# Transposing the attention weights of the last three batches by DMA instead of on TensorE

## The chip, the cores and the metric

The kernel runs on one core of one Trainium2 chip. The metric is the device time of one execution in microseconds (us), lower is better. Executions of one kernel differ by 1 to 2% here, a few by 3%, so kernels are compared only by runs taken in turn on the same chip, and only by those in the fast state (within 1.5% of the fastest of that kernel). A ratio is the mean time of one kernel's fast runs over that of the other's in the same rounds, so it is not quite the ratio of the medians that are quoted.

## The reference, cut to what matters

```python
# 8 batches, 8 heads, 576 positions, 64 channels a head; 32 packed queries a head
p_packed = softmax(p @ k.T / 8) @ v            # [8, 8, 32, 64]
attn = softmax(q @ p_packed.T / 8) @ p_packed  # [8, 8, 576, 64] -> x [8, 576, 512]
x1, x2, x3 = split(x @ w_proj)                 # gates x1, x3; x2 is convolved
y = x1 * irfft(rfft(x2) * rfft(filter)) * x3
out = y @ w_out                                # [8, 576, 512] float32
```

The softmax weights of the second attention (576 positions by 256 packed rows, a batch) are used twice: as they are for the convolution, and transposed for the gates x1 and x3.

## The kernel before: the parts that the change and the argument touch

Every operation is first recorded, then a planner inside the program simulates the engines and fixes the order of each engine's instructions before they are emitted. Its view of a DMA from SyncE (SP): 60 ns of the queue, and a landing some 3 us later. The batches run as a pipeline of four stages; `turn` makes the transposed weights `a2t` and `middle`, one stage later, uses them.

```python
def rates(self):
    if self.dma():
        return 760 if self.engine == "POOL" else 60, 4000 + self.transfer_ns()
...
def turn(b):                       # a2n: softmax product, 4 blocks; a2c: its tail
    ...
    for t in range(2):
        tp = pst(f"a2tp_b{b}", [P, S], FP16)                       # PSUM
        nc.tensor.transpose(tp[:, ds(COL0[4] - 64 * t, P)], a2c, ident[:])
        for i in range(4):
            ...
            nc.tensor.transpose(to, a2n[:, i, ts(t, P)], ident[:])
        nc.vector.tensor_copy(out=a2t[:, t, :], in_=tp[:])
...
def gate(*ms):                     # in middle(b)
    for x, c0 in ((x1, 0), (x3, 2 * DM)):
        for m in ms:
            for t in range(2):
                nc.tensor.matmul(x[:, m - ms[0], :], qm[:, t, ds(c0 + m * P, P)], a2t[:, t, cols],
                                 start=(t == 0), stop=(t == 1))
...
def project_out(n):                # in back(b): five os_b buffers, stores on SP
    ...
    os_ = sb([P, DM], FP32, tag="os", name=f"os_b{b}", bufs=5)
    nc.scalar.mul(out=os_[:], in_=o[:], mul=float(1.0 / SC_Y))
    nc.sync.dma_start(...)         # one to three stores
```

SP already carried four large transposes, those of the queries of batches 4 to 7 (`qT_b<-qn_b`, 16 blocks of 128x128 in one instruction), beside the stores.

The softmax here doesn't subtract the row's maximum and nothing guards it: scores larger than these inputs give would overflow.

## Time and profile before

| | before |
|---|---|
| time, median of three runs | 201.28 us (200.71 to 203.0) |
| span of the profiled execution | 198.3 us |
| PE busy | 184.8 us, 93% of the span |
| transposes of `a2t` on PE | 80, of them 30 in batches 5 to 7 |
| copies of `a2t` on DVE | 16, 0.45 us each |

PE is TensorE, DVE VectorE, ACT ScalarE, POOL GpSimd. The page, the stretches and the chain stand in the prediction below. Two lines are from the tile views of the kernel before, for `qT_b` and for `os_b`. The columns are the number of instructions, the shortest, median and longest time that one held SP (ns), and the first and last start (us).

```profile
L440 SPq DMA_TRANSPOSE qT_b<-qn_b x4: 1937/5840/10869, 73.7 to 112.8; - x4
L440 SPq DMA_DIRECT2D out_dram<-os_b x56: 330/413/772, 52.7 to 194.5; - x56
```

### The profile page before, as it was taken

The numbers are of one execution on the slowest core, as the hardware profiler recorded it, in microseconds if no ns is written. First come the engines' busy times: TensorE is split into PE (matmuls) and PEld (weight loads), VectorE is DVE, ScalarE is ACT, GpSimd is POOL, SyncE is SP. The second block draws the span as 40 slices with busy tenths as digits, with TensorE's granted clock in tenths as the row PEclk, the third lists the DMA queues.
The fourth block names the chain that finished last, engine by engine and source line by source line (L and its number), as shares of the span: only waits on it lengthen the run. The fifth ranks groups of instructions, "written<-read, shape, count | busy, mean of one in ns | idle before, by whom it ended". The sixth has DMA issues, their size and how long they took to land.

```text
span 198.3 us, 5799 instructions
## 1 busy us (share of the span) xinstructions
PE 184.8 (93%) x2413; PEld 114.7 (58%) x2413; DVE 142.2 (72%) x268; ACT 126.4 (64%) x265; POOL 133.5 (67%) x108
## 2 busy tenths in 40 slices
PE   4879989989999999999999999999999999999990
PEld 2226555666765775766665666565756465664630
DVE  4246857998369699966896699668966996798610
ACT  2247567597879978758874878478758556416050
POOL 7404578878566699989966996299529985963100
PEclk9999999999999999999999999999999999999996
DMA  5999999999999999889999999943013103503235
GB/s 136 270 269 197 205 207 198 196 199 195 202 217 268 189 201 179 165 116 244 263 173 156 112 126 201 172 130 85 3 55 107 56 0 118 143 10 132 81 126 141
DMA packets 44843, 30.96 MB, mean 156 GB/s; under 512 B 16336, under 2 KB 39376, under 8 KB 44816
## 3 DMA queue, kind: packets, MB, share of 16 engines
q0 software_dynamic: 29312, 16.52, 60.9%
q1 hardware_dynamic: 14784, 13.34, 28.9%
q10 hardware_dynamic: 720, 0.72, 1.2%
q8 instruction: 19, 0.31, 0.6%
q14 instruction: 8, 0.07, 0.1%
HBM read 35.55 MB, written 9.44 MB: 227 GB/s over the span
## 4 chain that ended last, share of the span: by engine, by line
PE 73%; DVE 8%; DMA 7%; POOL 4%; ACT 3%; issue 1%; ACTq 0%; DVEq 0%; POOLq 0%
PE x_b L440 28%; PE o_b L440 14%; PE f_b L440 7%; DMA kn_b<-in_k_dram 7%; PE fp_b L440 5%; PE s_b L440 4%; DVE tt_b L440 3%; PE kTp_b L440 3%; PE pv_b L440 3%; PE qp_b L440 3%; PE hp L440 2%; DVE zs_b L440 2%; PE a2tp_b L440 2%; PE qTp_b L440 1%; POOL gm_b L440 1%; POOL fa_b L440 1%
## 5 line engine op out<-in xcount | busy, mean ns | idle before, releaser
L440 POOL TENSOR_TENSOR gm_b<-tt_b,tt_b 128x512 f16<-128x512 f32 (+1 forms) x28 | 39.3, 1431 | 5.8 <-DVE tt_b L440 5.3
L440 DVE TENSOR_TENSOR tt_b<-f_b,h 128x1024 f32<-128x1024 f32 x32 | 38.7, 1214 | 4.7 <-PE f_b L440 4.1
L440 PE MATMUL x_b<-a2t_b,qm_b 128*128 128x512 f16 (+1 forms) x256 | 40.9, 286 | 0.2
L440 PE MATMUL x_b<-ac,gm_b 128*128 128x64 f16 (+3 forms) x312 | 36.0, 252 | 0.1
L440 ACT ACTIVATE os_b<-o_b 128x512 f32<-128x512 f32 x36 | 21.4, 597 | 21.8 <-PE o_b L440 21.8
L440 PE MATMUL o_b<-wout,y_b 128*128 128x512 f16 x128 | 33.4, 379 | 0.0
L440 ACT CAST qm_b<-qp_b 128x512 f16<-128x512 f32 x48 | 26.6, 590 | 10.6 <-PE qp_b L440 10.5
L440 POOL TENSOR_TENSOR tt_b<-tt_b,tt_b 128x1024 f32<-128x1024 f32 x12 | 28.3, 2360 | 5.0 <-DVE tt_b L440 4.9
L440 DVE TENSOR_TENSOR w_b<-x1s_b,x_b 128x512 f32<-128x512 f32 (+1 forms) x40 | 24.6, 627 | 8.9 <-ACT x1s_b L440 8.7
L440 ACT COPY x1s_b<-x_b 128x512 f32<-128x512 f32 (+1 forms) x40 | 21.9, 547 | 11.1 <-PE x_b L440 7.7
L440 PEld LDWEIGHTS <-gm_b 128*128 128x128 f16 x312 | 22.3, 98 | 8.8 <-POOL gm_b L440 2.6
L440 POOL TENSOR_TENSOR fa_b<-ez_b 128x512 f16<-128x512 f32 x14 | 17.6, 1273 | 14.2 <-ACT ez_b L440 14.2
L440 PE MATMUL f_b<-qm_b,fa_b 128*128 128x512 f16 x80 | 24.1, 379 | 0.4 <-DVE tt_b L440 0.2
L440 ACT ACTIVATE e_b<-s_b 96x384 f16<-96x384 f32 (+1 forms) x48 | 23.5, 533 | 1.1 <-PE s_b L440 1.0
L440 DVE SCALAR_TENSOR_TENSOR y_b<-w_b,x_b 128x512 f16<-128x512 f32 x32 | 20.6, 681 | 3.9 <-PE x_b L440 3.7
L440 PEld LDWEIGHTS <-a_b 128*128 128x128 f16 x240 | 15.9, 98 | 8.5 <-POOL a_b L440 1.2
L440 PEld LDWEIGHTS <-qm_b 128*128 128x128 f16 x256 | 15.7, 98 | 8.6 <-issue 1.1
L440 POOL TENSOR_TENSOR a_b<-e_b,zr_b 128x1152 f16<-128x1152 f16 (+2 forms) x10 | 17.3, 1735 | 3.5 <-ACT qm_b L440 2.4
L440 PEld LDWEIGHTS <-y_b 128*128 128x128 f16 x128 | 11.9, 98 | 11.5 <-DVE y_b L440 0.6
L440 PE MATMUL kTp_b<-ident,kn_b 96*128 96x96 f16 x192 | 13.0, 205 | 0.9 <-DVE tt_b L440 0.5
L440 PEld LDWEIGHTS <-kn_b 96*128 96x128 f16 x192 | 11.0, 97 | 4.7 <-issue 2.0
L440 ACT COPY ez_b<-fp_b 128x512 f32<-128x512 f32 x16 | 9.4, 586 | 3.7 <-PE fp_b L440 3.4
(78 smaller groups left out, 280.4 us busy)
## 6 DMA issues: line engine op xcount, KB each, us to landing
out_dram<-os_b SPq DMA_DIRECT2D x24, 256.0 KB, 2.7
kn_b<-in_k_dram POOLq DMA_DIRECT2D x8, 576.0 KB, 13.1
vn_b<-in_v_dram POOLq DMA_DIRECT2D x8, 576.0 KB, 14.8
qn_b<-in_q_dram POOLq DMA_DIRECT2D x8, 512.0 KB, 15.1
out_dram<-os_b SPq DMA_DIRECT2D x16, 128.0 KB, 2.4
wp<-in_moe_w_proj_dram POOLq DMA_DIRECT2D x3, 512.0 KB, 18.5
filt<-in_moe_filter_fft_dram SPq DMA_DIRECT2D x4, 256.0 KB, 6.6
out_dram<-os_b SPq DMA_DIRECT2D x16, 64.0 KB, 1.9
```

The source lines that it names most:

```text
L440: ins = op.call(*op.args, **op.kw).ins
```

## The change

The intent: take ten transposes and two copies per batch off the bound engine and VectorE in batches 5, 6 and 7, when the DMA engines have little to do. Each batch's weights are transposed by twelve DMAs on the SP queue.

```diff
-    TURNED = 4
+    TURNED, TURNED_K, TURNED_A = 4, 9, 5
...
-        for t in range(2):
+        for t in range(2) if b >= TURNED_A else ():
+            for i in range(4):
+                for r, c in ((slice(0, P), COL0[i]),) if i != 2 else ((slice(0, 64), 320), (slice(64, P), MAIN)):
+                    nc.sync.dma_start_transpose(a2t[:, t, c:c + r.stop - r.start], a2n[r, i, ts(t, P)])
+            nc.sync.dma_start_transpose(a2t[:, t, ds(COL0[4], 64)], a2c[64 * t:64 * t + 64, :])
+        for t in range(2) if b < TURNED_A else ():
             tp = pst(f"a2tp_b{b}", [P, S], FP16)
```

The rest of the diff offers the same for the keys from batch `TURNED_K` = 9 on, which no batch reaches.

More of the change, by code (lines that the diff above doesn't have):

```diff
@@ L665, in q_tail @@
                                       in_=tp[:, :, c].rearrange("p g (r e) -> p g e r", e=2))
-        k_turn(0)
-        yield 260
+        for g in range(4) if b >= TURNED_K else ():
+            nc.sync.dma_start_transpose(kTr[g][:, 0:6 * KP].rearrange("p (x r) -> p x r", r=KP),
+                                        kn[:, 2 * g:2 * g + 2, :].rearrange("p h x -> p (h x)"))
+        if b < TURNED_K:
+            k_turn(0)
+            yield 260
         pack()
         yield 230
-        k_turn(1)
-        yield 260
+        if b < TURNED_K:
+            k_turn(1)
+            yield 260
         score1(0)
         yield 270
-        k_turn(2)
-        yield 260
+        if b < TURNED_K:
+            k_turn(2)
+            yield 260
         score1(1)
         yield 270
-        k_turn(3)
-        yield 260
+        if b < TURNED_K:
+            k_turn(3)
+            yield 260
         score1(2)
```

## The prediction

> **What bounds the kernel now.** I first read the page: the totals by engine, the forty slices, the chain of work that ended last.
>
> ```profile
> PE 184.8 (93%) x2413; PEld 114.7 (58%) x2413; DVE 142.2 (72%) x268; ACT 126.4 (64%) x265; POOL 133.5 (67%) x108
> ...
> PE   4879989989999999999999999999999999999990
> ...
> PEclk9999999999999999999999999999999999999996
> DMA  5999999999999999889999999943013103503235
> ...
> PE 73%; DVE 8%; DMA 7%; POOL 4%; ACT 3%; issue 1%; ACTq 0%; DVEq 0%; POOLq 0%
> ```
>
> TensorE (PE) is busy in 93% of the span, at full clock, and from the fourth slice on it is hardly ever free; the chain that ends last runs through it for 73% of the time. The other engines have room on average. The DMA row matters too: the engines are full until about slice 26 (129 us), while the inputs are loaded, and almost idle after that.
>
> A busy figure does not say that PE is the limit exactly where the change acts, so I then cut the span at the starts of the softmax products (tile a_b: 117.8 us for batch 5, 137.5 for batch 6, 158.2 for batch 7, from the timeline of GpSimd).
>
> ```profile
> 97.40:117.80 20.40, 20.31 (x290) 13.02 (x289) 16.12 (x30) 15.08 (x34) 16.70 (x14) 1.00 1.35 158
> 117.80:137.50 19.70, 19.23 (x275) 12.34 (x275) 15.95 (x30) 13.79 (x30) 14.23 (x11) 1.00 0.76 150
> 137.50:158.20 20.70, 20.54 (x277) 12.62 (x275) 16.20 (x28) 14.54 (x32) 14.22 (x10) 1.00 0.16 52
> 158.20:176.70 18.50, 18.50 (x166) 11.59 (x166) 14.86 (x22) 8.49 (x16) 14.04 (x10) 1.00 0.25 74
> ```
>
> The columns are the stretch and its length, the busy time of PE, PE's weight loads, VectorE (DVE), ScalarE (ACT) and GpSimd (POOL), the clock, and the share and rate of DMA. In the stretches of batches 5 to 7 PE idles for 0.5, 0.2 and 0.0 us. So what leaves PE's queue there shortens the kernel by nearly its own length. There is one hole to fill: at 132.6 to 136.5 us the chain leaves PE for DVE.
>
> ```profile
> 132.17 0.45 PE f_b L440 x2
> 132.64 0.69 DVE gm_b L440
> 133.33 0.36 DVE a2t_b L440
> 133.69 1.27 DVE zs_b L440
> 135.02 0.26 issue
> 135.28 1.17 DVE tt_b L440
> 136.49 0.42 PE kTp_b L440 x6
> ```
>
> One of the copies that the change removes (a2t_b) stands in that piece of DVE work.
>
> **What the Trainium skill says.** (1) "TensorE: Matmul & The Clock Gate", Part 4: PE-mode transpose, gives about 390 ns for a 128x128 transpose alone and about 275 ns within a kernel, with a copy out of PSUM to follow. The trace has a mean of 219 ns here, but that is its length from start to end; back to back, only the distance between starts counts, and it is 56 ns (below). The measurement decides. (2) "VectorE: DVE Perf Modes", The three transpose paths, puts the DMA way at 1309 ns for 128x128. No run yet has such a piece alone; the trace has four large ones. (3) "DMA: Bandwidth & Descriptors", Rules for kernel authors, says that transfers under 64 KB pay mostly overhead. The pieces are 32 KB and 16 KB. The trace agrees as far as it goes: output stores of 64 to 256 KB all hold the SP queue for about 0.4 us and land after some 2 us. (4) The same page, DMA Transpose (X-bar), warns of two queues transposing at once; here every one is on SP, so nothing is added to serialize them.
>
> **The change part by part.** The line with TURNED_K = 9 is inert, since no batch number reaches 9; the keys stay on PE. Only the three batches 5, 6 and 7 of the attention weights move.
>
> ```profile
> L440 PE MATMUL a2tp_b<-ident,a_b 128*128 128x128 f16 x80 | 7.4, 219 | 0.0
> L440 DVE COPY a2t_b<-a2tp_b 128x576 f16<-128x576 f16 x16 | 7.1, 450 | 4.4 <-PE a2tp_b L440 4.4
> qT_b<-qn_b SPq DMA_TRANSPOSE x4, 10.9
> ```
>
> Removed from PE: ten transposes per batch, thirty in all. In the PE timeline a group of five starts at 132.44 and the next matmul at 132.72, so five cost 0.28 us and one 56 ns. Thirty times 56 ns is 1.7 us, all in stretches where PE is the limit.
>
> Removed from DVE: two copies per batch, six in all; 6 x 0.45 is 2.7 us of DVE. DVE is some 80% busy in these stretches, so most of that is worth nothing; I count only the hole, 0.36 us on the chain for batch 5. Two PSUM banks per batch come free as well, which I count as nothing.
>
> Added on SP: twelve transposes per batch, 36 in all. What one holds SP is an estimate: an output store holds it 0.41 us in the median, and the one whole-batch transpose that ran after the others' traffic had eased took 1.94 us for 16 blocks of 128x128, 0.12 us a block. So a piece takes some 0.33 + 0.12 = 0.45 us, twelve take 5.4 us. That same large transpose landed 4.3 us after its start, 2.4 us after SP had issued it. Hence all twelve have landed about 7.8 us after the first is issued. The DMA engines' own work is small: it moved 512 KB in about 4 us; a batch is 288 KB.
>
> Is this hidden? For each batch I compare the end of the softmax product with the first gate matmul that reads a2t. Batch 5: product done at 119.9, but SP is held by the last query transpose until 123.65; 123.7 + 7.8 is 131.5, with five output stores of 0.4 us in between 133.5; needed at 137.3. Batch 6: 139.6 + 7.8 is 147.4; needed at about 155.5. Batch 7: 160.3 + 7.8 is 168.1; needed at 171.7. All three have slack, 3.8, 8 and 3.6 us, so the latency lies beside other work.
>
> Moved: the emitted order of all instructions is planned by the program itself before it is built, so removing operations reshuffles it, perhaps from the start. The planner takes 60 ns of SP and a landing some 3 us after the start for such a piece, less than I estimate.
>
> Added on PE: the gate matmuls now wait on several DMA completions instead of one DVE copy; the completions rotate over few semaphores (the trace shows eight for SP). Where an instruction cannot carry all its waits, extra semaphore instructions stand before it. If six per batch cost 50 ns each (what they cost SP in this trace) and none is hidden, that is 0.9 us over three batches; I expect half, 0.4 us.
>
> Sum: -1.7 (PE) - 0.4 (hole) + 0.4 (waits) = -1.7 us. The base is 201.3 us as a median of three that lie 2.3 us apart; the profiled execution took 200.05 us. I take 201.2 as the base and predict 199.5 us.
>
> **Rivals.** First, the pieces land late and the gates wait for them. For it: the query transposes landed after 14 and 18 us while inputs were being loaded, and the plan assumes quicker pieces than I do, so it may pull gates to where their data is not yet there. Against it: DMA is at 0.16 and 0.25 of capacity in batches 6 and 7, and the last load lands at 123 us, before batch 5's pieces can start. It would cost 1 to 3 us in each of one or two batches and make 201 to 205 us.
>
> Second, SP becomes the bound: stores stand behind twelve pieces, the five os_b buffers fill, ScalarE waits and PE with it. For it: 5.4 us of SP in one block, and each issue waits for the landing of the eighth before it. Against it: SP is idle for 8 to 10 us in each stretch (135.5 to 145.9, 153.8 to 163.8), just after the products end, and one batch fills only four or five os_b buffers. It would make 200 to 203 us.
>
> Third, more gain than the instructions removed: with a2t ready 2 to 5 us earlier and without PSUM, gate matmuls can fill holes such as that of 132.6 to 136.5 us. In the three stretches PE has 0.7 us free and perhaps 1 us more in the last 22 us, so it would make 198 us, hardly less.
>
> Fourth, pieces into one tile are held one after another, each waiting for the landing of the one before: 12 x 2.4 us is 29 us per batch and the end would slip by 15 to 20 us. Against it: the second query transpose was issued at 79.4, before the first had landed at 81.1, and the pieces write disjoint columns. I give it 3%.
>
> **Range and chances.** A change of -1.7 us is -0.8%, and the medians themselves wander by half a per cent. Rival three sets the low end, 198.0; rivals one and two the high end, 202.3. Faster by over 2% needs 197.2 us, more than twice the PE time removed: 6%. Slower by over 2% needs 205.3, a stall in two batches or rival four: 7%. The rest, 87%, is within 2%.
>
> **What would show it.** PE should have 2383 matmuls less any change in filler ones, with ten a2tp transposes in each of batches 0 to 4 only, and DVE ten a2t copies instead of sixteen. SP should show 40 transposes, 36 of them about 0.45 us long, landing within 2 to 3 us. The stretch between softmax products should be about 0.5 us shorter in the last batches. I am wrong if the waits list PE behind a DMA into a2t_b for more than 1 us, if pieces hold SP far longer than 0.45 us, or if ScalarE's os_b waits for SP's stores. If the time falls by 3 us or more, the worth of PE's 56 ns was not the main term.

## The result, and the profile after

| | before | after |
|---|---|---|
| median | 201.0 us | 212.35 us (210.08 to 215.02) |
| ratio of the fast runs | | 1.0527, 95% interval 1.0414 to 1.0639 |

The kernel became 5% slower, outside the stated range. The first profile fell in the slow state (215.0 us), so the changed kernel was run once more, unedited, for a profile of a fast execution: 210.29 us, beside 210.1 us of the two fastest runs above. All lines of the changed kernel are of that second profile. What stood on record for it:

> The changed kernel once more, unedited, for a profile in the fast state (the one in hand is of the slow state, 215.0 us). Expected 210 to 212 us, SP held 1.22 us by each of the 36 pieces, 15 us per batch, PE waiting for a2t three times for 8 to 10 us in all, and the granted clock at half in one stretch after each wait over 3 us. If the wait for a2t is absent in a fast run, the slow state explained the wait and not the change.

The page: busy times, then PE, the clock granted to it and the DMA engines in forty slices, and the chain that ended last.

```profile
PE 187.5 (90%) x2383; PEld 114.8 (55%) x2383; DVE 140.1 (67%) x262; ACT 126.5 (61%) x265; POOL 133.5 (64%) x108
...
PE   4889989999999999999999969998994799799990
...
PEclk9999999999999999999999988999999589999997
DMA  5999999999999999999999995113601341047325
...
PE 50%; SPq 18%; DMA 10%; DVE 8%; POOL 5%; ACT 3%; issue 3%; ACTq 0%; DVEq 0%; POOLq 0%
```

The counts are as predicted: PE has 2383 matmuls in place of 2413, DVE 262 instructions in place of 268. The order that the planner gave PE is unchanged for its first 1737 matmuls. But PE now has holes late in the kernel, the clock falls there, and SP's queue, absent from the chain of before, holds 18% of it. The DMA engines themselves have room there (0.58, 0.29 and 0.25 of capacity in the stretches below). The same cut as in the prediction, at the softmax products of this run (117.5, 140.9 and 161.7 us; the last stretch ends where batch 7's gates have found their data), with the columns named there:

```profile
117.50:140.90 23.40, 20.78 (x265) 12.68 (x264) 15.71 (x28) 14.56 (x32) 14.22 (x11) 0.93 0.58 98
140.90:161.70 20.80, 17.42 (x250) 10.63 (x250) 14.33 (x24) 13.34 (x29) 14.23 (x11) 0.99 0.29 78
161.70:182.00 20.30, 17.77 (x125) 9.48 (x125) 11.45 (x16) 7.90 (x15) 11.56 (x8) 0.85 0.25 68
```

PE was free for 0.5, 0.2 and 0.0 us in the stretches of before; here it is free for 2.6, 3.4 and 2.5 us. Who released it, from the view of waits (total, times, longest):

```profile
PE x_b L440 <- DMA a2t_b<-a_b: 6.4, 3, 4.1
```

That is a gate matmul waiting for the transposed weights, once in each of the three batches (6.4 us in all, less than the 8 to 10 that were expected). Why they are late stands in SP's queue: how long a piece holds it (tile view of `a2t_b`), and its order in time (start, length, what).

```profile
L440 SPq DMA_TRANSPOSE a2t_b<-a_b x36: 1121/1226/2130, 125.7 to 182.1; - x36
```

```profile
125.72 17.01 SPq L440 DMA_TRANSPOSE a2t_b<-a_b  x12
142.83 5.23 SPq L440 DMA_DIRECT2D out_dram<-os_b  x8
148.60 15.68 SPq L440 DMA_TRANSPOSE a2t_b<-a_b  x12
164.39 3.12 SPq L440 DMA_DIRECT2D out_dram<-os_b  x6
167.62 15.68 SPq L440 DMA_TRANSPOSE a2t_b<-a_b  x12
```

A piece holds SP for 1.23 us in the median, not 0.45, whether it has 128 rows or 64, and twelve hold it for 16 to 17 us. From 125.7 to 183.3 us SP is never free for longer than 0.6 us: from one batch's first piece to the next batch's it takes 22.9 and 19.0 us, where the kernel before had 19.7 and 20.7 us for a batch in all. So pieces are late for the gates, and they begin late too: those of batch 5 behind a query transpose, those of batches 6 and 7 behind the stores of the batch before.

The waits cost more than their length. "TensorE: Matmul & The Clock Gate", Why this matters for your kernels, in the Trainium skill, says that a gap of more than about 3 us between matmuls sends TensorE back to the slow clock. The longest wait of this trace agrees: from 161.1 us on, within the wait of 4.1 us that ends at 163.0, the clock is granted at one half for 6.8 us, while in the kernel before it fell only at the very end. (Not every gap agrees; see pieces_unused and the last section.) The columns are those of the stretches above; the clock is the third from the end.

```profile
161.12:167.94 6.82, 4.97 (x24) 2.33 (x25) 0.69 (x1) 1.66 (x3) 2.70 (x2) 0.50 0.39 118
```

Not all of this profile's loss is shown to be the change's: at 120.7 us PE idles for 1.9 us for no reason that the profile names, and 3.4 us at half clock follow; this gap is most of the 2.6 us of the first stretch above. The slow profile of the same kernel has no such gap, but waits of 9.9 us for `a2t` and three stretches of 3.4 us at half clock, each beginning between 0.5 us before and 1.4 us after the end of such a wait.

An estimate from these numbers: 6.4 us of waits, 2.5 us for the work done at half clock after them (half of 4.97), 1.9 us of the unexplained gap and 1.7 us for the half clock after it make 12.5 us. The span grew by 10.1 us although some 1.5 us of work was taken away (nothing_added below), so 11.6 us are to be explained.

### The profile page after: what moved, and what is told of

The parts are those of the page before. It is cut to its first block, busy times and chain, and to the rows that moved or that the text cites.

```text
span 213.2 us, 5781 instructions
## 1 busy us (share of the span) xinstructions
PE 188.9 (89%) x2383; PEld 115.7 (54%) x2383; DVE 140.1 (66%) x262; ACT 126.3 (59%) x265; POOL 133.4 (63%) x108
## 4 chain that ended last, share of the span: by engine, by line
PE 51%; SPq 20%; DMA 9%; DVE 7%; POOL 5%; ACT 3%; issue 2%; ACTq 0%; DVEq 0%; POOLq 0%
PE x_b L440 20%; SPq L440 20%; PE o_b L440 8%; DMA kn_b<-in_k_dram 7%; PE f_b L440 4%; PE s_b L440 3%; PE fp_b L440 3%; PE kTp_b L440 3%; DVE tt_b L440 3%; DMA a2t_b<-a_b 2%; POOL tt_b L440 2%; PE hp L440 2%; PE qp_b L440 2%; PE pv_b L440 2%; PE qTp_b L440 1%
## 5 line engine op out<-in xcount | busy, mean ns | idle before, releaser
L440 PE MATMUL x_b<-a2t_b,qm_b 128*128 128x512 f16 (+1 forms) x256 | 42.9, 291 | 9.9 <-DMA a2t_b<-a_b 9.9
L440 PE MATMUL x_b<-ac,gm_b 128*128 128x64 f16 (+3 forms) x312 | 38.9, 264 | 0.1
L440 PEld LDWEIGHTS <-gm_b 128*128 128x128 f16 x312 | 23.8, 102 | 10.6 <-issue 2.4
L440 POOL TENSOR_TENSOR fa_b<-ez_b 128x512 f16<-128x512 f32 x14 | 17.6, 1269 | 13.9 <-ACT ez_b L440 13.9
L440 PE MATMUL f_b<-qm_b,fa_b 128*128 128x512 f16 x80 | 24.8, 387 | 0.4 <-DVE tt_b L440 0.2
L440 PEld LDWEIGHTS <-a_b 128*128 128x128 f16 x210 | 13.8, 98 | 7.3 <-POOL a_b L440 1.2
L440 PE MATMUL kTp_b<-ident,kn_b 96*128 96x96 f16 x192 | 14.5, 217 | 1.0 <-DMA kn_b<-in_k_dram 0.5
L440 PEld LDWEIGHTS <-kn_b 96*128 96x128 f16 x192 | 12.1, 104 | 5.4 <-issue 2.6
```

What stands on the lines that cost most here:

```text
L440: ins = op.call(*op.args, **op.kw).ins
```

## The experiments

Twelve runs; nothing_added gave wrong output. The medians are of all runs, the ratios of the fast ones to those of the kernel before, in the same rounds.

| run | edit | median us | ratio (95% interval) |
|---|---|---|---|
| sizes | kernel before, ten DMAs after its end | 227.0 | - |
| nothing_added | transposes taken away, none put in | 198.91 | 0.9927 (0.9877 to 0.9977) |
| merged7 | seven pieces for twelve | 198.46 | 0.9927 (0.9857 to 0.9996) |
| pieces_unused | pieces issued, result not used | 206.16 | 1.0321 (1.0249 to 1.0392) |
| after_again | changed kernel | 210.29 | one run |
| only_last | batch 7 alone | 204.09 | 1.0170 (1.0083 to 1.0258) |
| kept_warm | PE kept busy in the waits | 208.27 | 1.0396 (1.0325 to 1.0466) |
| told_plan | planner told 1270 ns | 208.82 | 1.0414 (1.0322 to 1.0506) |
| stores_on_act | stores issued by ScalarE | 228.16 | 1.1341 (1.1252 to 1.1430) |
| whole | one transpose per batch, 5 to 7 | 198.93 | 0.9941 (0.9915 to 0.9968) |
| whole_from4 | the same from batch 4 | 198.35 | 0.9929 (0.9903 to 0.9956) |
| whole_from1 | the same from batch 1 | 202.58 | 1.0130 (1.0091 to 1.0169) |

The theory, A: a transposing DMA costs SP a fixed time per instruction, so twelve small pieces fill SP's queue, and everything behind it is late. Rivals are named with each run.

### What one transpose costs SP (sizes)

```diff
+    nc.vector.tensor_copy(out=scr[:, 0:DM], in_=last[0][:])        # scr, dst: dead query tiles
+    for n in (1, 1, 2, 4, 8, 9, 16):
+        nc.sync.dma_start_transpose(dst[:, 0:n, :], scr[:, 0:n * P])
+    nc.sync.dma_start_transpose(dst[:, 0, 0:64], scr[0:64, 0:P])
+    nc.sync.dma_start_transpose(dst[:, 0, 0:32], scr[0:32, 0:P])
+    nc.sync.dma_start(dst[:, 0, :], scr[:, 0:P])
```

> The kernel before with ten further DMAs on SP after its last store, one at a time (all write one dead tile, so each waits for the landing of the one before): transposes of 1, 1, 2, 4, 8, 9 and 16 blocks of 128x128, then one of 64 rows, one of 32 rows, and a plain copy of 128x128. It is there to be measured, not to be fast (some 30 us longer). Theory A (a fixed cost per transposing instruction): the one-block pieces hold SP 1.1 to 1.25 us, the 64-row and the 32-row one as long, nine blocks 1.4 to 1.7 us, sixteen 1.9 us. Rival B (cost by the block): one block 1.2 us, two 2.4 us, sixteen far over the 1.94 us seen in the kernel before, or else the 64-row piece half of the 128-row one. Rival C (back-pressure by earlier pieces in flight): alone, one block takes 0.4 to 0.5 us and only pieces in a row take 1.2 us. The plain copy: 0.35 to 0.5 us in all theories.

From SP's timeline (start, time that it holds SP): one block, eight blocks, sixteen blocks, one block of 32 rows, and the plain copy.

```profile
200.01 1.10 SPq L440 DMA_TRANSPOSE qn_b<-qn_b  x1
207.07 1.23 SPq L440 DMA_TRANSPOSE qn_b<-qn_b  x1
213.39 1.32 SPq L440 DMA_TRANSPOSE qn_b<-qn_b  x1
219.97 1.10 SPq L440 DMA_TRANSPOSE qn_b<-qn_b  x1
222.23 0.51 SPq L440 DMA_DIRECT2D qn_b<-qn_b  x1
```

Sixteen times the work costs SP 0.2 us more, and a quarter of the rows nothing less. The cost is by the instruction: some 1.1 us, against 0.5 us for a plain copy of the same bytes. It is there with no other piece in flight, so back-pressure (rival C) isn't needed. Nor is there a cost by the block that matters (rival B); I had expected more for the large ones, 1.4 to 1.7 us for nine blocks and 1.9 us for sixteen, and nine took 1.28. This is the cost while nothing else moves. In the kernel before, sixteen blocks held SP for 1.94 to 10.9 us while inputs were being loaded; what makes that excess no run shows. They landed 2.2 us after their start for one block, 3.1 for eight, 4.3 for sixteen, 1.8 for the plain copy. What SP does in that 1.1 us the trace doesn't show.

### What the removal is worth (nothing_added)

```diff
-            a2t = s["a2t"] = sb([P, 2, S], FP16, tag="a2t", name=f"a2t_b{b}")
+            a2t = s["a2t"] = wt if b >= TURNED_A else sb([P, 2, S], FP16, tag="a2t", name=f"a2t_b{b}")
...  (and the DMA transposes left out)
```

> Wrong results on purpose: in batches 5 to 7 the transposes on PE and the copies on DVE are gone and no DMA takes their place; the gates read a constant that has long been loaded. It shows what the removal alone is worth. The prediction's term: 30 x 56 ns on PE and 0.36 us of DVE, 1.7 to 2.1 us, so a ratio of 0.990 to 0.992. If the removal is worth nothing (rival E), 1.000; if early gates fill holes, 0.985.

The ratio 0.9927 is 0.7%, some 1.5 us of 200.5. The gain side of the prediction, 1.7 to 2.1 us before the waits, is right to within the interval (0.5 to 2.5 us). All four compute engines have exactly the order of the changed kernel, so the new order isn't what costs: the loss comes from what was added.

### Fewer instructions, the same bytes (merged7)

```diff
-        for t in range(2) if b >= TURNED_A else ():
-            for i in range(4):
+        for i in range(4) if b >= TURNED_A else ():
...
-                    nc.sync.dma_start_transpose(a2t[:, t, c:c + r.stop - r.start], a2n[r, i, ts(t, P)])
+                    nc.sync.dma_start_transpose(a2t[:, :, c:c + r.stop - r.start], a2n[r, i, :])
```

> The changed kernel with both halves t of a column block in one instruction: 7 transposes per batch in place of 12, the same bytes, the same order on PE. Theory A (fixed cost by the instruction): 7 x 1.3 us is 9 us of SP per batch in place of 15.2, the gates of batch 5 find their data or wait under 0.5 us, those of 6 and 7 too, and the time is 199 to 201 us. Rival B (cost by the block or byte): SP is held 15 us as before and the time stays at 209 to 211 us.

SP's timeline:

```profile
125.25 10.88 SPq L440 DMA_TRANSPOSE a2t_b<-a_b  x7
136.23 4.99 SPq L440 DMA_DIRECT2D out_dram<-os_b  x8
141.35 9.19 SPq L440 DMA_TRANSPOSE a2t_b<-a_b  x7
```

SP is held 9 to 11 us in place of 16 to 17, and no wait of PE for `a2t` is left in the view of waits. All four compute engines have exactly the order of the changed kernel, only SP's differs, and the time falls from 5% above the kernel before to 0.7% below it, the whole worth of the removal. This decides between the instruction and the byte.

### SP's occupancy without the gates' wait (pieces_unused)

```diff
-                    nc.sync.dma_start_transpose(a2t[:, t, c:c + r.stop - r.start], a2n[r, i, ts(t, P)])
+                    nc.sync.dma_start_transpose(spare[:, t, c:c + r.stop - r.start], a2n[r, i, ts(t, P)])
...  (spare is a dead query tile; transposes on PE and copies on DVE stay)
```

> The 36 pieces are issued as in the changed kernel, but into a dead tile that nobody reads, and the transposes on PE and the copies on DVE stay: PE, DVE and ACT have the order of the kernel before. Theory A (the gates' wait for late pieces is what costs): the time is that of the kernel before, 200 to 202 us, though SP is held 15 us per batch. Rival D (SP's occupancy: output stores stand behind the pieces, buffers fill, ScalarE and PE wait): 205 to 210 us, with os_b waiting for stores.

Here I had expected the time of the kernel before, and was wrong: 3.2% slower, although no gate reads the pieces and PE, DVE and ACT have the order of the kernel before. From the view of waits:

```profile
ACT os_b L440 <- DMA out_dram<-os_b: 6.0, 2, 5.3
PE x_b L440 <- ACT os_b L440: 3.3, 1, 3.3
```

ScalarE waits for an output buffer whose store stands behind twelve pieces, and PE waits for ScalarE. So rival D is true as well. The two ways are not simply to be added: both are made of the same time on SP, and in the changed kernel's fast profile PE waits at the gates and not for an output buffer. The profile is of the fastest of these runs (203.41 us); how the other two fast runs lost some 2.6 us more it doesn't show.

The clock did not fall after this wait of 3.3 us (181.5 to 184.85 us), which is longer than some after which it fell elsewhere (the same columns, first the wait, then what follows):

```profile
181.50:184.90 3.40, 0.07 (x2) 0.05 (x1) 0.31 (x1) 0.65 (x2) 2.34 (x1) 1.00 0.60 198
184.90:190.00 5.10, 5.10 (x44) 3.06 (x44) 2.43 (x5) 2.39 (x5) 0.00 (x0) 1.00 0.93 280
```

### One batch alone (only_last)

```diff
-    TURNED, TURNED_K, TURNED_A = 4, 9, 5
+    TURNED, TURNED_K, TURNED_A = 4, 9, 7
```

> The changed kernel with only batch 7 moved to DMA. SP is idle when batch 7's softmax product ends at 160.3 us, so twelve pieces run to 175.6 and land by 176.8; the gates are planned at 171.1 to 171.7. One wait of 4 to 5 us for a2t, less 0.56 us of PE saved, with at most 1.7 us lost to the clock: 203 to 206 us. If a backlog of three batches is needed to do harm (rival H), 200 to 201 us.

```profile
PE x_b L440 <- DMA a2t_b<-a_b: 3.0, 1, 3.0
```

Within the stated range: 1.7%, about 3.4 us, from one wait of 3.0 us, and 3.4 us at half clock from 175.1 us on, in a batch that found SP free. No backlog is needed (rival H is out).

### The clock's part (kept_warm)

```diff
+            if b >= TURNED_A and ms == (0,):
+                for _ in range(16):
+                    nc.tensor.matmul(x1[:, 0, :], qm[:, 0, 0:P], wout[:, 0, :], start=True, stop=True)
```

> The changed kernel with 16 matmuls of 512 columns (3.5 us of PE, their results are overwritten) ahead of the first gate of batches 5, 6 and 7, so that PE works while it would wait for a2t. The results stay right. Theory A with a clock term: in the profile in hand each wait of 2.8 to 3.9 us is followed by a stretch of 3.4 us at half clock, worth up to 1.7 us each; kept busy, the clock stays at 1.0 and, as the wait hides the 10.4 us of added matmuls, the time is 206 to 209 us, below the changed kernel's 210 to 212. If the clock does not matter, the time is 210 to 213; if the waits were not there, 220.

```profile
PEclk9999999999999999999999999999999999999999
```

The 48 matmuls are 10.4 us of work that serves nothing, and the kernel with them was faster than the one run of the changed kernel beside it, 208.27 to 210.29 us. The clock stays full, and PE no longer waits for `a2t`. So working through the waits was some 2 us cheaper than idling through them. That this is the fallen clock's price is argued, not shown: the intervals of the two ratios overlap (1.0325 to 1.0466 and 1.0414 to 1.0639), and the planner gave PE, DVE and ACT a somewhat different order. The estimate from the trace above, 2.5 us after the waits, is of the same size.

### Was it the plan (told_plan)

```diff
-            return 760 if self.engine == "POOL" else 60, 4000 + self.transfer_ns()
+            hold = 760 if self.engine == "POOL" else 1270 if "a2t" in self.out.tensor.name else 60
+            return hold, 4000 + self.transfer_ns()
...  (and the same where the planner issues)
```

> The changed kernel, whose planner is told that such a piece holds SP for 1270 ns in place of 60 ns. The order of all engines changes, from the start. Theory F (SP is nearly full: 12 x 1.27 us of pieces and 8 stores of 0.45 us are 18.8 us of a stretch of 19.7 us, so no order hides it): 205 to 211 us. Rival G (the plan alone was at fault, because it put the gates where it wrongly believed the data to be): 199 to 202 us.

```profile
PE x_b L441 <- DMA a2t_b<-a_b: 7.0, 3, 3.9
```

Told the pieces' cost (stores still count 60 ns in it), this planner finds no order that hides it: 208.82 us, with three waits as before (the profile is of the slow state). That fits theory F and speaks against G; other orders were not tried, so that none would do is not shown. The plan did not change from the start, as I had expected: PE's order is that of the changed kernel for the first 1729 of 2383 matmuls, and differs after that.

### Stores moved off SP (stores_on_act)

```diff
-                nc.sync.dma_start(rows[...], os_[:])
+                (nc.scalar if b >= 2 else nc.sync).dma_start(rows[...], os_[:])
```

> The changed kernel with the output stores of batches 2 to 7 issued by ScalarE, so that SP has nothing but pieces in these batches and no store stands behind a piece (34 stores of about 0.45 us go to ScalarE, which is busy in 61% of the span). It separates the gates' own wait from SP's backlog. If the gates' wait for a2t alone makes the loss, twelve pieces still take 15.2 us: batch 7's, begun at the product's end at 160 us, land by 178, some 6 us after the gates' place in the plan; two or three waits of 1 to 5 us remain and the time is 204 to 209 us. If most of the loss is stores and pieces standing behind each other, 199 to 202 us. Over 210 us would mean that ScalarE cannot bear the stores, and then it tells nothing.

This one failed to answer its question, as the last sentence allows. But the reason isn't that ScalarE has no time:

```profile
ACT x1s_b L440 <- DMA a2t_b<-a_b: 10.7, 2, 8.6
ACT qm_b L440 <- DMA a2t_b<-a_b: 7.5, 1, 7.5
```

ScalarE, which has no business with `a2t`, waits for the pieces' landing. In this program the DMAs that SP and ScalarE issue take their completion semaphores from one set of eight in turn (numbers 107 and 109 to 115 in this trace, for both), so a store on ScalarE waits until a piece that had the same semaphore has landed. A slow queue thus stops a compute engine. How much of the changed kernel's loss the stores standing behind pieces would make by themselves stays open; that it comes from what was put on SP's queue does not.

### A version that keeps the gain (whole, whole_from4, whole_from1)

All nine blocks of a batch go into one instruction, and the gates read them where they land, each matmul of 512 columns cut into four.

```diff
-        (twelve transposes)
+        if b >= TURNED_A:
+            nc.sync.dma_start_transpose(a2t[:], s["a2"][:])     # a2t: [128, 9, 128]
...
+            even = a2t[:, 0:8, :].rearrange("p (a e t) r -> p a e t r", a=2, e=2)
+            return [(x[:, 0:256]..., [even[:, :, 1, t, :] for t in range(2)]),
+                    (x[:, 256:320], [a2t[:, 8, 64 * t:64 * t + 64] for t in range(2)]), ...]
```

> One transpose per batch in batches 5 to 7: all nine blocks of the softmax product, its tail with them, into a tile of nine blocks, and the gates read the blocks where they lie, each matmul of 512 columns cut into four (48 more matmuls per batch[...]). Theory A: SP is held 1.3 us per batch in place of 15.2, a2t lands some 3.2 us after the product, nothing waits, and the time is that of the removal alone (ratio 0.993) with at most 0.3 us on top: ratio 0.990 to 0.996, the same as with seven pieces or better. If the cutting of the gates costs what the transposes cost, 1.000.

> The same from batch 4 on. Batch 4's product ends at 99.5 us, while inputs are loaded and the query transposes hold SP 6.8 and 10.9 us; its a2t may land 10 to 15 us after the product, and its gates begin some 16 us after it. Another 0.5 us gained, ratio 0.987 to 0.995, if it lands in time; over 0.995 if not.

> The same from batch 1 on. In batches 1 to 3 the DMA engines are full with input loads (landings of 12 to 18 us), and batch 1 has the least time between product and gates. If all land in time 7 x 0.5 us is 3.5 us, ratio 0.983; I expect late landings in one or two batches and a ratio of 0.99 to 1.02.

For batches 5 to 7 SP is held 1.3 to 2.3 us per batch and nothing waits: 0.9941. Cutting the gates costs little: by the distances between starts in this trace, the four parts take 109, 29, 29 and 57 ns, 224 in place of 216. From batch 4 on the time is 0.9929, the best of these by the median of its rounds and not to be told apart from the first or from seven pieces by the intervals. Both are faster than the kernel before by 0.6 to 0.7%, with an interval clear of 1. From batch 1 on it is 1.3% slower:

```profile
PEld L440 <- DMA a2t_b<-a_b: 3.3, 2, 2.4
PE x_b L440 <- DMA a2t_b<-a_b: 3.0, 2, 2.3
```

In batches 1 and 2, whose product is transposed while inputs are loaded, the one transpose held SP for only 1.7 us but landed 11 us after its start, and the gates waited 0.75 and 2.29 us, with 3.4 us at half clock after the second. The rest of its loss was not traced.

## Why the prediction was wrong

**What bounds the kernel** was right. PE is the limit in those stretches: taking its transposes away and adding nothing gave 0.7%, about the 1.7 us that 30 x 56 ns make.

**The step that failed** is "What one holds SP is an estimate", whose outcome was "a piece takes some 0.33 + 0.12 = 0.45 us, twelve take 5.4 us". It took the fixed part from a plain store and laid the whole 1.94 us on sixteen blocks, 0.12 us each. (The 1.94 us itself was too much: with nothing else moving, sixteen blocks took 1.32.) The measured division is the other way round: 1.1 us fixed for a transposing instruction and 0.014 us a block ((1.32 - 1.10) / 15). In a row, pieces start 1.27 us apart, so twelve take 15.2 us or more. The figure of 1309 ns from the page that the prediction cited was nearer to this than my estimate; I passed it over because no run had such a piece alone.

With that one term put right, the comparison in the same paragraph gives the result: pieces of batch 7 from 160.3 us on have landed by 160.3 + 15.2 + 2.4 = 177.9, and are needed at 171.7. For batch 5, 123.7 + 17.6 = 141.3 against 137.3. For batch 6, 139.6 + 17.6 = 157.2 against 155.5. "All three have slack" is false for all three, even without the stores. (The 2.4 us after SP's issue are the prediction's, from sixteen blocks; a small piece lands 1.2 us after its issue, which makes 176.7, 140.1 and 156.0, still late.)

**Rivals.** The first (late pieces, 201 to 205 us) is what happened, in all three batches in place of one or two. It was set aside by looking at the idle DMA engines; the queue that issues was the limit, not the engines that move. The second (SP becomes the bound) is true too, by pieces_unused; "SP is idle for 8 to 10 us in each stretch" was right (10.4 and 10.1 us), and less than the 15 us that were needed. The third was not needed: nothing_added gained no more than the instructions removed. The fourth did not occur; a piece is issued before the one before it has landed.

**Not in the prediction at all** was the clock: no rival spoke of what an idle PE costs after its wait. It is some 2 us, by an estimate from the trace and by kept_warm, which doesn't isolate it.

**Waits on PE.** The prediction's 50 ns is what such an instruction takes on PE (51 ns in the trace), not on SP as it says (17 ns there). I guessed six extra semaphore instructions per batch. The trace has 12 more in all (23 in place of 11), so four. Since merged7 has six more in all and reaches the time of nothing_added, what they cost is not seen.

## What to carry to other kernels

Before moving work from a compute engine to a DMA queue, multiply the number of instructions by the time that one of that kind holds the issuing queue, and compare the sum, stores included, with the time of one stage; idle DMA engines don't show that there is room. Where the queue's cost is by the instruction, put all blocks of a batch into one and let the consumer read them where they land. Test a queue's cost with the smallest piece at the end of a working kernel before building on an estimate from another kind of DMA.

## What the Trainium skill lacked or had wrong

- "DMA: Bandwidth & Descriptors" (DMA Transpose (X-bar), Rules for kernel authors) has no figure for how long one small SBUF-to-SBUF transpose holds the issuing queue, by its size, on this chip; its one table of sequencer cycles has, for earlier generations, only small transposes out of HBM and one of 8,192 tiles. Measured: 1.10 to 1.32 us for one to sixteen blocks of 128x128, 1.10 us for 32 rows, 0.51 us for a plain copy. Its rule that small transfers pay mostly overhead is right, and doesn't say that this overhead blocks the stores behind.
- "VectorE: DVE Perf Modes" (The three transpose paths) has 1309 ns for the DMA way. Here a block holds the queue 1.10 to 1.23 us and has landed 2.2 us after its start; the page doesn't say which of the two is meant, and nine blocks cost the queue hardly more than one.
- "TensorE: Matmul & The Clock Gate" (Part 4: PE-mode transpose) gives 275 to 390 ns, lengths of one transpose (219 ns here from start to end). It doesn't say that a busy PE pays only the distance between starts, 56 ns here in an unbroken stream; Part 1 of the page has that distance for ordinary matmuls.
- The same page (Why this matters for your kernels) puts the gap that brings back the slow clock at about 3 us. Here the length alone did not decide: gaps of 1.9 us (after_again) and 2.3 us (whole_from1) were followed by 3.4 us at half clock, gaps of 2.4 us (told_plan), 2.6 us (stores_on_act) and 3.3 us (pieces_unused) were not, and all of 3.9 us and more were.
